# A weight conversion laid out as a pipeline, with batch 0's convolution and some residuals moved to the matrix engine

## The chip, the core and the metric

The kernel runs on one core of a Trainium2 chip. Five engines work beside each other, each through its own queue in order: PE (TensorE, matmuls and their weight loads, shown as PEld), DVE (VectorE), ACT (ScalarE), POOL (GpSimd) and SP (SyncE, here only a queue that issues DMAs). ACT's queue issues DMAs too. The time that counts is the device time of one execution in microseconds. Three runs of the kernel before gave 1051.89, 1057.13 and 1061.42 us; the median is 1057.13 us.

## The reference, cut to what matters

Three stages follow each other, for 4 batches of 576 positions and 512 channels:

```python
scores = scale * np.matmul(q, k.transpose(0, 1, 3, 2))          # 8 heads of 64
kth = np.partition(scores, -32, axis=-1)[..., -32:-31]           # the 32nd largest of each row
attn = softmax(np.where(scores >= kth, scores, -1e9))
x = concat_heads(attn @ v)                                       # (4, 576, 512)

gate = sigmoid(sum(conv_w[k] * xp[:, k:k+S, :] for k in range(5)))   # causal, per channel
x = (gate * (x @ w_val)) @ w_out

u = x + real(fft(fft(x, axis=1), axis=2))
un = layernorm(u)
out = u + relu(un @ w_ch1) @ w_ch2                               # 512 -> 2048 -> 512
```

The five weights (w_val, conv_w, w_out, w_ch1, w_ch2) come as 64-bit floats. The kernel reads them as pairs of 32-bit words and builds a 32-bit float out of each pair; every matrix is then split into a 16-bit high part and a 16-bit low part (the residual), so that three 16-bit matmuls replace one in 32 bits.

## The kernel before, in words

Attention is worked off pair of heads by pair of heads: 16 pairs (4 for each batch), each in five tiles u = 0 to 4 of 128 query rows for two heads (the fifth tile holds both heads' last 64 rows). For a tile PE computes the scores into PSUM (`pss`, L219), ACT copies them out (`ssb`, L220 and L221), and DVE finds the 32 largest of each row: five instructions on halves (L245 to L249), then four rounds of MAX8 (L260) with three of MATCH_REPLACE8 (L269) between them. ACT takes the exponential (L265), DVE masks it by the threshold (L283, one tile later), ACT writes the high part `hl` (L284), and the low part comes from POOL (L285, L292), except that in batch 0 512 of 576 columns of it come from PE: the identity `eye` times the 32-bit e minus the identity times the 16-bit hl (`pe`, L288 and L289), copied out by ACT (L290). A transposing DMA on SP turns hl into `et` (L294), and PE multiplies it with v into `pav` (L316).

At the end of a pair (`attn_finish`) PE spreads the row sums (`pr`, `pt`), ACT copies them (`xt`, L353, L354), DVE normalises (L355), and the causal convolution with five taps follows for the pair's 128 channels: ACT makes the nearest and the farthest tap (L358, L363), DVE adds three taps (L369, 3 instructions in the first three pairs of a batch), POOL adds the farthest (L371, through the helper of L117), and ACT takes the tanh (L372). ACT also copies x out for the following matmul (`xhl` L364, `xt` L365).

Beside attention run, in the slots of the tiles, other units of work: during batch 0 the conversion of the weights (`prelude_units`), during batch b+1 the rest of batch b (`moe_units`); the rest of batch 3 comes last, alone. Each unit of the prelude gets a slot by its position in a list.

The conversion of one unit of 1024 floats in each of 128 partitions: ACT's queue issues the load of 1 MB (L668 or L670) into one of two raw buffers (`bx_pre`, `bz_pre`); two DVE instructions put the mantissa and exponent into `ub`, one of two places in `bx_pre` (L671, L672); ACT makes the sign (L675) and the absolute value (L678); POOL multiplies both in four pieces (L685 to L686 through L117). `wsplit` then adds the split: ACT writes the high part (L692), PE forms the low part as above (`pl`, L697 and L698, two halves), and ACT copies it out (L699). 18 units go through `wsplit` (2 of w_val, 8 of w_ch1, 8 of w_ch2); w_out goes through `p1` with its low part by POOL (L736), and its folded copy `wsd` by POOL as well (L747). conv_w goes through `p0`: its load on SP (L718), three small instructions on DVE (L725, L726, L730) and two on ACT (L728, L729).

The unit's code is written out in one piece: load, mantissa, sign, product, split. The framework's scheduler then orders each engine's instructions by program position and by a time model of its own, puts in the waits, and so moves instructions across each other. A wait on one instruction stops all that stand behind it on that engine.

## Time and profile before

| | |
|---|---|
| median of three runs | 1057.13 us |
| the profiled execution | 1057.91 us |
| its span, first to last instruction | 1054.4 us |
| busy in the span: PE, DVE, ACT, POOL | 881.2, 846.2, 664.3, 565.4 us |
| batch 0's attention with the weight conversion | to about 275 us |
| batches 1, 2, 3 | to about 475, 683, 887 us |
| the rest of batch 3, alone | 887 to 1054 us |

The stages are read from the reciprocal that ends each fourth pair's row sums (L334 and L335 at 275.1, 479.9, 687.5 and 888.1 us). Busy time of an engine is an average over stages with different limits, so the prediction looks at the stage that is changed, from 0 to 275 us, by its own table of windows.

### The profile page before, as it was taken

The page shows a single profiled execution, that of the slowest core. Times are in us where ns is not written, and L with a number is a line of the kernel's source. Part 1 is how long each engine was busy: PE and PEld are TensorE (multiplying, and loading weights), DVE is VectorE, ACT ScalarE, POOL GpSimd, SP SyncE. Part 2 cuts the span into 40 slices and gives each one's busy share as a digit, 9 for nine tenths or more (in the row PEclk, how much of TensorE's full clock was granted, in tenths as well). Part 3 has the DMA queues.
Part 4 walks back from the last instruction along what each step waited for, and adds up shares of the span by engine and source line. Part 5 has one row for each costly group of instructions (what it writes and reads, how often), then busy time and mean ns, then how long its engine had stood idle before and what let it go on. Part 6 is the DMA issues. An engine that isn't in the chain of part 4 may idle for free.

```text
span 1054.4 us, 21240 instructions
## 1 busy us (share of the span) xinstructions
PE 881.2 (84%) x7282; PEld 513.4 (49%) x7282; DVE 846.2 (80%) x2568; ACT 664.3 (63%) x1394; POOL 565.4 (54%) x806
## 2 busy tenths in 40 slices
PE   1277767866789799898998998979979998899996
PEld 0033233322455565544656555446555564558563
DVE  5987979968898999998899998999998997223120
ACT  5587987868756877766669758565785763323020
POOL 1764652524485766755957658559584663641000
PEclk9977888988999999998999999999989999999999
DMA  7698585766536555555364546664464353301000
GB/s 205 162 269 222 128 189 129 181 109 131 103 63 105 97 113 120 100 125 123 82 122 93 116 97 110 138 141 70 99 111 91 83 108 55 80 21 26 21 2 29
DMA packets 308805, 115.18 MB, mean 109 GB/s; under 512 B 297040, under 2 KB 300880, under 8 KB 306384
## 3 DMA queue, kind: packets, MB, share of 16 engines
q1 hardware_dynamic: 303840, 90.24, 43.8%
q10 hardware_dynamic: 4848, 23.50, 6.8%
q8 instruction: 59, 0.97, 0.4%
q14 instruction: 58, 0.48, 0.2%
HBM read 44.49 MB, written 6.82 MB: 49 GB/s over the span
## 4 chain that ended last, share of the span: by engine, by line
DVE 32%; PE 27%; ACT 14%; DMA 12%; issue 6%; POOL 6%; SPq 2%; ACTq 0%; POOLq 0%; DVEq 0%
DVE e L283 7%; PE ph L579 6%; DMA et<-hl 5%; PE po L602 5%; DVE tc L260 5%; DVE ty L269 4%; PE pv L407 3%; DMA stk<-pre 3%; DVE ty L249 2%; POOL hl L292 2%; PE pav L316 2%; ACT hl L284 2%; ACT ssb L220 2%; ACT e L265 2%; PE pd L461 2%
## 5 line engine op out<-in xcount | busy, mean ns | idle before, releaser
L260 DVE MAX8 tc<-ty 128x8 f32<-128x96 f32 (+3 forms) x576 | 229.8, 432 | 2.5 <-DVE e L283 0.5
L579 PE MATMUL ph<-R_un,w 128*128 128x256 f16 (+1 forms) x1536 | 202.3, 290 | 14.0 <-ACT bx_h L583 6.5
L579 PEld LDWEIGHTS <-w 128*128 128x128 f16 x1536 | 148.4, 99 | 62.8 <-issue 21.0
L219 PE MATMUL pss<-stk 128*128 128x512 f16 (+3 forms) x640 | 95.0, 306 | 74.3 <-DVE ty L249 45.0
L284 ACT ACTIVATE hl<-e 128x576 f16<-128x576 f32 x144 | 97.9, 683 | 92.6 <-DVE e L283 70.0
L283 DVE SCALAR_TENSOR_TENSOR e<-ssb,tc,e 128x576 f32<-128x576 f32 x144 | 139.4, 996 | 2.6 <-ACT e L265 2.4
L269 DVE MATCH_REPLACE8 ty<-tc,ty 128x144 f32<-128x144 f32 (+2 forms) x432 | 137.2, 323 | 0.0
L602 PE MATMUL po<-w2f,bx_h 128*128 128x512 f16 x576 | 129.2, 379 | 0.0
L316 PE MATMUL pav<-et,vhl 128*64 128x128 f16 (+1 forms) x2240 | 95.2, 224 | 38.7 <-DMA et<-hl 36.9
L292 POOL TENSOR_TENSOR hl<-e,hl 128x512 f16<-128x512 f32 x108 | 125.0, 1157 | 0.0
L265 ACT ACTIVATE e<-ssb,ngm 128x576 f32<-128x576 f32 x144 | 107.4, 777 | 3.9 <-PE pe L288 1.4
L316 PEld LDWEIGHTS <-vhl 128*64 128x64 f16 x2240 | 72.1, 115 | 77.1 <-issue 72.7
L285 POOL TENSOR_TENSOR hl<-e,hl 128x64 f16<-128x64 f32 x144 | 47.5, 333 | 104.6 <-ACT hl L284 82.3
L163 POOL TENSOR_TENSOR pre<-r,pre 96x384 f16<-96x384 f32 x60 | 60.7, 1020 | 79.5 <-ACT r L162 66.8
L219 PEld LDWEIGHTS <-stk 128*128 128x128 f16 (+1 forms) x640 | 41.4, 104 | 124.3 <-issue 76.2
L602 PEld LDWEIGHTS <-bx_h 128*128 128x128 f16 x576 | 55.1, 98 | 64.9 <-issue 0.6
L220 ACT COPY ssb<-pss 128x1024 f32<-128x1024 f32 (+1 forms) x80 | 73.4, 918 | 10.4 <-PE pss L219 7.9
L580 ACT ACTIVATE bx_h<-ph 128x256 f16<-128x256 f32 (+1 forms) x96 | 38.7, 409 | 55.4 <-PE ph L579 55.2
L407 PE MATMUL pv<-xhl,R_wv 128*128 128x288 f16 x384 | 55.9, 303 | 13.1 <-ACT xt L353 5.0
L156 ACT ACTIVATE pre<-r 96x384 f16<-96x384 f32 x60 | 29.6, 519 | 44.6 <-DMA stk<-pre 16.5
L249 DVE TENSOR_TENSOR ty<-pss,ssb 128x576 f32<-128x576 f32 (+1 forms) x80 | 55.6, 695 | 1.9
L697 PE MATMUL pl<-bx_pre,U_wp 128*128 128x512 f32 x72 | 45.4, 716 | 12.0 <-ACT hl L290 6.4
(186 smaller groups left out, 1705.3 us busy)
## 6 DMA issues: line engine op xcount, KB each, us to landing
bx_pre<-in_moe_w_ch_dram ACTq DMA_DIRECT2D x8, 1024.0 KB, 5.7
bz_pre<-in_moe_w_ch_dram ACTq DMA_DIRECT2D x8, 1024.0 KB, 5.3
r<-in_q_dram SPq DMA_DIRECT2D x32, 144.0 KB, 2.7
r<-in_k_dram SPq DMA_DIRECT2D x31, 144.0 KB, 2.6
stk<-stk SPq DMA_DIRECT2D x60, 72.0 KB, 2.3
vr<-in_v_dram SPq DMA_DIRECT2D x32, 128.0 KB, 2.7
out_dram<-U_u SPq DMA_DIRECT2D x16, 256.0 KB, 2.4
R_wv<-scr_wv SPq DMA_DIRECT2D x3, 1024.0 KB, 5.1
```

The lines of the kernel that those rows point to most:

```text
L219: mm(pss[pr, bank, cs], stk[:, 2 * vv, qs], stk[:, 1, ks], start=(vv == 0), stop=(vv == 1))
L220: nc.scalar.copy(ssb[:, :g, 0:512], pss[:, :g, :])
L260: last = vec.max(out=c[:, cols[i], 8 * r : 8 * r + 8], in_=src[:, i, w])
L265: act(e, ssb[:, i, :], AF.Exp, bias=ngm[:, i : i + 1], scale=SC_EXP)
L269: vec.match_replace(out=y[:, i, w], in_to_replace=c[:, cols[i], 8 * r : 8 * r + 8], in_values=src[:, i, w], imm_value=-1e30,)
L283: done = vec.scalar_tensor_tensor(e, ssb[:, i, :], thr, e, op0=ALU.is_ge, op1=ALU.mult, accum_out=rsum)
L284: act(hl[:, 0:S], e, AF.Copy, bias=0.0, scale=1.0)
L292: pool.tensor_tensor(hl[:, S + D : 2 * S], e[:, 0:512], hl[:, 0:512], op=ALU.subtract)
L316: av = mm(st["pav"][i * D : (i + 1) * D, qs], vhl[:, hv, i, cv, :], rhs, start=(m == 0), stop=(m == len(steps) - 1),)
L407: mm(pv[:, :HS], a, r, start=(n == 0), stop=(n == len(pairs) - 1))
L579: mm(ph[:, :nt], a, r, start=(i == 0), stop=(i == len(pr) - 1))
L602: mm(po, a, r, start=(f == 0 and i == 0), stop=(f == NF - 1 and i == 2))
```

## The change

The conversion is split into `raw_load`, `mant`, and `finish`, and a list `weights` of the 18 units is walked by `wstep(n)`: it issues the split of unit n-1, then mantissa, sign and product of unit n, then the load of unit n+1. There are 19 steps where there were 18 units. In `p1` and `p2` POOL's subtractions give way to `pe_lo`: two matmuls and a copy by ACT for each 512 columns, eight times in all. The three small DVE instructions on conv_w move, in the program, from ahead of `p2` to behind the second `wstep` (`p0b`). In batch 0, for the first three pairs, `attn_finish` makes five diagonal matrices of the taps by ACT, in place of the two tap instructions, and lets PE sum the five shifted products in PSUM (`pc`, 512 and 64 columns), from which ACT takes the tanh in two pieces; the three instructions of DVE and the two of POOL go.

```diff
         vec.tensor_tensor(x, x, xt, op=ALU.mult)
         g = e1[:, hp, :]
         last = KC - 1
+        if b == 0 and hp < NPAIR - 1:
+            dg = [e1[:, hp + 1, j * P : (j + 1) * P] for j in range(last)] + [state[("m", 0)]["dg"]]
+            for j in range(KC):
+                act(dg[j], eye, AF.Copy, bias=0.0, scale=cw[:, hp, j : j + 1])
+            act(xhl[:, 0], x, AF.Copy, bias=0.0, scale=1.0)
+            nc.scalar.copy(xt, x)
+            pool_tt(xhl[:, 1], xt, xhl[:, 0], op=ALU.subtract)
+            for n0, n1 in ((0, 512), (512, S)):
+                pc = ps_m.tile([P, 512], F32, tag="psm", name=f"pc_{hp}_{n0}")
+                for j in range(last, -1, -1):
+                    lo = max(n0, last - j)
+                    mm(pc[:, lo - n0 : n1 - n0], dg[j], xt[:, lo - last + j : n1 - last + j], start=(j == last), stop=(j == 0))
+                act(g[:, n0:n1], pc[:, 0 : n1 - n0], AF.Tanh, bias=0.0, scale=0.5 / SX)
+            return
         act(g, x, AF.Copy, bias=0.0, scale=cw[:, hp, last : last + 1])
         far = 0
         if hp < NPAIR - 1:
...
+        def raw_load(src):
+            raw = (blk["z"] if i else blk["t"])[:, 0:2048].bitcast(I32)
...
                 nc.scalar.dma_start(raw.rearrange("p (c n) -> p c n", c=src.shape[1]), src)
             else:
                 nc.scalar.dma_start(raw, src)
+            words = raw.rearrange("p (n t) -> p n t", t=2)
+            tops = raw.bitcast(F16).rearrange("p (n t) -> p n t", t=4)[:, :, 3]
+            return words, tops, blk["t"][:, 2048 + i * 1024 : 3072 + i * 1024]
+        def mant(words, ub):
+            ui = ub.bitcast(I32)
             vec.tensor_scalar(ui, words[:, :, 1], 3, 0x40000000, op0=ALU.logical_shift_left, op1=ALU.bitwise_xor)
             vec.scalar_tensor_tensor(ui, words[:, :, 0], 29, ui, op0=ALU.logical_shift_right, op1=ALU.bitwise_or)
+        def from_f64(src, ub, scale):
+            words, tops, _ = raw_load(src)
+            mant(words, ub)
+            act(words[:, :, 0], tops, AF.Tanh, bias=0.0, scale=SIGN_SCALE)
             act(ub, ub, AF.Abs, bias=0.0, scale=1.0)
-            if dst is None:
-                pool_tt(ub, ub, sg, op=ALU.mult, parts=4)
-            elif 2 <= blk["n"] <= 4:
+            if blk["n"] == 2:
...
-        def wsplit(src, dst_h, dst_l, scale):
-            ub = from_f64(src, None, 1024, scale)
-            u3 = ub.rearrange("p (c n) -> p c n", c=src.shape[1]) if len(src.shape) == 3 else ub
+        weights = []
+
+        def wstep(n):
+            if n > 0:
+                finish(*weights[n - 1])
+            if n < len(weights):
+                ent = weights[n]
+                words, tops, ub = ent[4]
+                mant(words, ub)
+                sg = words[:, :, 0].bitcast(F32)
+                act(sg, tops, AF.Sign, bias=0.0, scale=1.0)
+                act(ub, ub, AF.Abs, bias=0.0, scale=1.0)
+                pool_tt(ub, ub, sg, op=ALU.mult, parts=4)
+            if n + 1 < len(weights):
+                weights[n + 1].append(raw_load(weights[n + 1][0]))
+
+        def finish(src, dst, scale, then, bufs):
+            ub = bufs[2]
+            dst_h, dst_l = dst()
+            u3 = ub.rearrange("p (c n) -> p c n", c=src.shape[1]) if three_d else ub
             act(dst_h, u3, AF.Copy, bias=0.0, scale=scale)
             for g in range(2):
                 pl = ps_m.tile([P, 512], F32, tag="psm", name=f"pl_{blk['n']}_{g}")
-                mm(pl, state[("m", 0)]["ident"] if scale == 16.0 else state[("m", 0)]["idw2"], ub[:, g * 512 : g * 512 + 512], start=True, stop=False)
+                mm(pl, state[("m", 0)]["ident" if scale == 16.0 else "idw2"], ub[:, gs], start=True, stop=False)
                 mm(pl, state[("m", 0)]["nid"], hs, start=False, stop=True)
                 act(ls, pl, AF.Copy, bias=0.0, scale=1.0)
+            if then:
+                then()
+
+        def pe_lo(dst, full, hi, name):
+            pl = ps_m.tile([P, 512], F32, tag="psm", name=name)
+            mm(pl, eye, full, start=True, stop=False)
+            mm(pl, neye, hi, start=False, stop=True)
+            act(dst, pl, AF.Copy, bias=0.0, scale=1.0)
...
+        def p0b():
...
             act(wohl[:, sl], woF[:, sl], AF.Copy, bias=0.0, scale=1.0)
-            pool.tensor_tensor(wohl[:, 2048 + 1024 * i : 3072 + 1024 * i], woF[:, sl], wohl[:, sl], op=ALU.subtract)
+            for g in range(2):
+                cs = slice(1024 * i + 512 * g, 1024 * i + 512 * g + 512)
+                pe_lo(wohl[:, 2048 + cs.start : 2048 + cs.stop], woF[:, cs], wohl[:, cs], f"po_{i}_{g}")
...
             act(wsd[:, :, 0, :], wt, AF.Copy, bias=0.0, scale=1.0)
-            for i in range(2):
-                sl = slice(2 * i, 2 * i + 2)
-                pool.tensor_tensor(wsd[:, sl, 1, :], wt[:, sl, :], wsd[:, sl, 0, :], op=ALU.subtract)
+            for c in range(NCC):
+                pe_lo(wsd[:, c, 1, :], wt[:, c, :], wsd[:, c, 0, :], f"pt_{c}")
...
+        for i in range(2):
+            src = w_val[256 * i : 256 * i + 256].rearrange("(c p) n -> p c n", p=P)
+            weights.append([src, lambda i=i: wv_dst(i), SWV, wv_save if i else None])
+        for dc in range(NCC):
+            for i in range(2):
+                src = w_ch1[dc * P : (dc + 1) * P, i * 2048 : (i + 1) * 2048]
+                ns = slice(i * 1024, (i + 1) * 1024)
+                weights.append([src, lambda dc=dc, ns=ns: (w1[:, dc, 0, ns], w1[:, dc, 1, ns]), SW1, None])
+        for fp in range(NF // 2):
+            src = w_ch2[fp * 256 : fp * 256 + 256].rearrange("(f p) n -> p f n", p=P)
+            fs = slice(2 * fp, 2 * fp + 2)
+            weights.append([src, lambda fs=fs: (w2[:, fs, 0, :], w2[:, fs, 1, :]), SW2, None])
...
         us.append((0, pi))
-        us.append((1, lambda: pv(0)))
-        us.append((1, lambda: pv(1)))
+        for n in range(2):
+            us.append((1, lambda n=n: wstep(n)))
+        us.append((0, p0b))
         us.append((0, pd))
+        for n in range(2, 11):
+            us.append((1, lambda n=n: wstep(n)))
         for ec in range(NCC):
             us.append((1, lambda ec=ec: p3(ec)))
-        for fp in range(NF // 2):
+        for n in range(11, 19):
+            us.append((1, lambda n=n: wstep(n)))
         return us
```

How the change moves instructions, at the three places that the prediction speaks of. First POOL, early in batch 0, around the output weight (w2f holds it, `pre`, `vhl` and `hl` belong to attention, w_80 is the buffer of w1 and holds the folded copy). Before:

```order
L117 TENSOR_TENSOR w2f<-w2f,bx_pre 128x256 x4
L163 TENSOR_TENSOR pre_2_219<-r_0_2_152,pre_2_219 96x6x64
L163 TENSOR_TENSOR pre_2_219<-r_0_2_154,pre_2_219 96x6x64
L741 TENSOR_TENSOR w_80<-w2f 128x4x255
L742 TENSOR_TENSOR w_80<-w2f 128x4x255
L736 TENSOR_TENSOR w2f<-w2f 128x1024
L199 TENSOR_TENSOR vhl_1_314<-vr_2_230,vhl_1_314 128x320
L736 TENSOR_TENSOR w2f<-w2f 128x1024
L285 TENSOR_TENSOR hl_0_0_0_257<-e_0_0_0_178,hl_0_0_0_257 128x64
L285 TENSOR_TENSOR hl_0_0_1_267<-e_0_0_1_180,hl_0_0_1_267 128x64
```

After the change:

```order
L117 TENSOR_TENSOR w2f<-w2f,bx_pre 128x256 x4
L163 TENSOR_TENSOR pre_2_233<-r_0_2_152,pre_2_233 96x6x64
L163 TENSOR_TENSOR pre_2_233<-r_0_2_154,pre_2_233 96x6x64
L788 TENSOR_TENSOR w_80<-w2f 128x4x255
L789 TENSOR_TENSOR w_80<-w2f 128x4x255
L199 TENSOR_TENSOR vhl_1_337<-vr_2_244,vhl_1_337 128x320
L285 TENSOR_TENSOR hl_0_0_0_271<-e_0_0_0_178,hl_0_0_0_271 128x64
L285 TENSOR_TENSOR hl_0_0_1_281<-e_0_0_1_180,hl_0_0_1_281 128x64
```

The two subtractions of L736 are gone, and the two of L747, which stood right behind these rows, too. DVE's rows at this place are the same in both: the first instruction on conv_w (L725, now L770) stands behind the last one on w_out and ahead of the second tile's L246.

Second DVE, around the fifth tile of the first pair (`ty_0_4`; the rows that read `bx_pre` or `bz_pre` are the conversion). Before:

```order
L260 MAX tc_0_137<-ty_0_4_588 128x8
L269 MATCH_REPLACE ty_0_4_588<-tc_0_137,ty_0_4_588 128x96
L260 MAX tc_0_137<-ty_0_4_588 128x8
L269 MATCH_REPLACE ty_0_4_588<-tc_0_137,ty_0_4_588 128x144
L671 TENSOR_SCALAR bx_pre<-bx_pre 128x1024
L260 MAX tc_0_137<-ty_0_4_588 128x8
L672 SCALAR_TENSOR_TENSOR bx_pre<-bx_pre 128x1024
L269 MATCH_REPLACE ty_0_4_588<-tc_0_137,ty_0_4_588 128x288
L297 TENSOR_REDUCE tc_0_137<-tc_0_137 128x9
L260 MAX tc_0_137<-ty_0_4_588 128x8
L671 TENSOR_SCALAR bx_pre<-bz_pre 128x1024
L672 SCALAR_TENSOR_TENSOR bx_pre<-bz_pre,bx_pre 128x1024
```

After the change:

```order
L283 SCALAR_TENSOR_TENSOR e_0_3_0_513,sums_0_138<-ssb_0_3_351,tc_0_137,e_0_3_0_513 128x576
L688 TENSOR_SCALAR bx_pre<-bz_pre 128x1024
L689 SCALAR_TENSOR_TENSOR bx_pre<-bz_pre,bx_pre 128x1024
L283 SCALAR_TENSOR_TENSOR e_0_3_1_515,sums_0_138<-ssb_0_3_351,tc_0_137,e_0_3_1_515 128x576
L260 MAX tc_0_137<-ty_0_4_608 128x8
L269 MATCH_REPLACE ty_0_4_608<-tc_0_137,ty_0_4_608 128x96
L260 MAX tc_0_137<-ty_0_4_608 128x8
L269 MATCH_REPLACE ty_0_4_608<-tc_0_137,ty_0_4_608 128x144
L260 MAX tc_0_137<-ty_0_4_608 128x8
L269 MATCH_REPLACE ty_0_4_608<-tc_0_137,ty_0_4_608 128x288
L260 MAX tc_0_137<-ty_0_4_608 128x8
L245 TENSOR_TENSOR pss_1_0_597<-pss_1_0_597,ssb_1_0_596 128x288
```

Counted through the list (w_out's two are 0 and 1, w_val's 2 and 3), units 6 and 7 had their mantissa instructions inside this tile. After, unit 5 stands ahead of it, and units 6 and 7 follow in the next tile and the one behind that. The rest of the 18 stays within about one tile of its old place, and the last stands in the fourth tile of the fourth pair in both.

Third PE, at the end of the first pair, while the second pair's tiles run (`pt` ends the row sums, `pe_1` and `pl` are low parts, `pss_1_4` is the score of the second pair's fifth tile). Before:

```order
L350 MATMUL pt_0_936<-neye,rsh_0_916 64x64
L288 MATMUL pe_1_0_994<-e_1_1_0_832,eye 128x512
L289 LDWEIGHTS neye
L289 MATMUL pe_1_0_994<-hl_1_1_0_990,neye 128x512
L288 MATMUL pe_1_1_1004<-e_1_1_1_834,eye 128x512
L289 LDWEIGHTS neye
L289 MATMUL pe_1_1_1004<-hl_1_1_1_1000,neye 128x512
L697 MATMUL pl_0_1039<-bx_pre,U_wp_387 128x512
L219 LDWEIGHTS stk_2_226
L219 MATMUL pss_1_4_1077<-stk_2_226 64x512
```

After the change:

```order
L219 LDWEIGHTS stk_3_592
L219 MATMUL pss_1_4_1108<-stk_3_592 64x64
L369 MATMUL pc_0_974<-xt_0_961,R_wv_409 128x512
L369 MATMUL pc_0_974<-xt_0_961,e_0_932 128x511
L369 MATMUL pc_0_974<-xt_0_961,e_0_932 128x510
L369 MATMUL pc_0_974<-xt_0_961,e_0_932 128x509
L369 MATMUL pc_0_974<-xt_0_961,e_0_932 128x508
L369 MATMUL pc_512_981<-xt_0_961,R_wv_409 128x64
L369 MATMUL pc_512_981<-xt_0_961,e_0_932 128x64 x4
L288 MATMUL pe_1_0_1025<-e_1_1_0_852,eye 128x512
L289 LDWEIGHTS neye
L289 MATMUL pe_1_0_1025<-hl_1_1_0_1021,neye 128x512
```

The ten matmuls of the convolution stand right behind the fifth tile's scores, ahead of the low parts of that pair's second tile, which stood ahead of those scores before. The same is found at the ends of the second and third pairs.

## Rows read from the trace of the kernel before

**Rows 1.** Table of windows: busy us and (instructions), granted clock, DMA share.
```profile
core 0: us, PE busy (x) PEld busy (x) DVE busy (x) ACT busy (x) POOL busy (x), PEclk, DMA share, GB/s
...
42.00:275.00 233.00, 166.31 (x977) 73.41 (x978) 201.84 (x573) 188.47 (x325) 114.44 (x159) 0.84 0.72 165
275.00:475.00 200.00, 177.65 (x1682) 110.35 (x1681) 188.15 (x610) 141.84 (x321) 130.78 (x184) 0.99 0.54 103
475.00:683.00 208.00, 193.43 (x1756) 119.19 (x1756) 194.89 (x620) 144.14 (x323) 139.17 (x197) 0.96 0.54 109
683.00:887.00 204.00, 186.47 (x1692) 113.52 (x1687) 192.93 (x619) 134.75 (x303) 127.93 (x185) 0.97 0.48 96
887.00:1054.00 167.00, 153.01 (x1170) 95.50 (x1168) 39.53 (x104) 36.34 (x90) 35.52 (x59) 0.99 0.15 33
```

**Rows 2.** Waits of DVE, 42 to 275 us: total, times, longest.
```profile
DVE bx_pre L671 <- PE pl L697: 15.9, 4, 7.4
DVE bx_pre L671 <- DMA bx_pre<-in_moe_w_ch_dram: 5.2, 2, 4.0
...
DVE e L369 <- ACT xt L365: 1.1, 1, 1.1
```

**Rows 3.** Waits of PE, 42 to 275 us.
```profile
PE pav L316 <- DMA et<-hl: 18.5, 7, 7.1
```

**Rows 4.** Timeline, 24 to 43 us: start, us, instruction, count.
```profile
26.78 0.20 ACT L728 ACTIVATE w<-w 128x20 int32<-128x20 f16 x1
...
28.25 2.77 POOL L163 TENSOR_TENSOR pre<-r,pre 96x384 f16<-96x384 f32 x2
...
29.30 10.90 DVE L725 TENSOR_SCALAR cw<-w 128x20 int32<-128x20 int32 x1
...
30.98 2.34 POOL L741 TENSOR_TENSOR w<-w2f 128x1020 f32<-128x1020 f32 x1
...
33.27 1.99 POOL L742 TENSOR_TENSOR w<-w2f 128x1020 f32<-128x1020 f32 x1
35.23 2.12 POOL L736 TENSOR_TENSOR w2f<-w2f 128x1024 f16<-128x1024 f32 x1
37.30 0.79 POOL L199 TENSOR_TENSOR vhl<-vr,vhl 128x320 f16<-128x320 f32 x1
38.05 2.12 POOL L736 TENSOR_TENSOR w2f<-w2f 128x1024 f16<-128x1024 f32 x1
...
40.12 0.45 DVE L246 TENSOR_TENSOR ty<-pss,ssb 128x288 f32<-128x288 f32 x1
```

**Rows 5.** Groups by line, 16 to 275 us: count | busy, mean ns | idle before.
```profile
L369 DVE SCALAR_TENSOR_TENSOR e<-pav,cw,e 128x575 f32<-128x575 f32 (+2 forms) x9 | 7.3, 809 | 1.1 <-ACT xt L365 1.1
...
L290 ACT ACTIVATE hl<-pe 128x512 f16<-128x512 f32 x34 | 20.1, 600 | 3.3 <-PE pe L289 3.3
...
L363 ACT ACTIVATE e<-pav,cw 128x572 f32<-128x572 f32 x3 | 2.3, 755 | 0.0
L358 ACT ACTIVATE e<-pav,cw 128x576 f32<-128x576 f32 x3 | 2.2, 750 | 0.0
```

**Rows 6.** Timeline of PE and DVE, at 146 and 223 to 229 us.
```profile
146.54 1.02 PE L697 MATMUL pl<-bx_pre,U_wp 128*128 128x512 f32 x2
147.40 0.38 PE L698 MATMUL pl<-w,U_wp 128*128 128x512 f16 x1
...
223.32 0.85 PE L316 MATMUL pav<-et,vhl 128*64 128x128 f16 x12 [7.11 <-DMA et<-hl]
...
224.99 2.08 PE L697 MATMUL pl<-bx_pre,U_wp 128*128 128x512 f32 x2
226.86 0.63 PE L698 MATMUL pl<-w2f,U_wp 128*128 128x512 f16 x1
...
229.22 0.69 DVE L671 TENSOR_SCALAR bx_pre<-bz_pre 128x1024 int32<-128x1024 int32 x1 [7.41 <-PE pl L697]
```

**Rows 7.** Groups of PE by form, 42 to 275 us.
```profile
L219 PE MATMUL pss<-stk 128*128 128x64 f16 x60 | 13.3, 222 | 0.0
```

**Rows 8.** Timeline of ACT at the start: a copy of the identity.
```profile
2.24 0.29 ACT L783 ACTIVATE U_wp<-eye 128x128 f32<-128x128 f32 x1
```

More of the change, by code (lines that the diff above doesn't have):

```diff
@@ L378, in moe_begin @@
         wvt = mp.tile([P, 2304], F32, tag="R", name=f"R_wv_{b}")
+        st["dg"] = wvt[:, NRW : NRW + P]
         st["wvv"] = wvt[:, :NRW].bitcast(F16).rearrange("p (c h n) -> p c h n", c=NCC, h=2)
@@ L652, in prelude_units @@
         blk = {"n": 0}
-        def from_f64(src, dst, n, scale):
+        def raw_load(src):
             i = blk["n"] % 2
@@ L659, in from_f64 @@
                 blk["z"] = mp.tile([P, NBZ], F32, tag="bz", name="bz_pre")
-            raw = (blk["z"][:, 0 : 2 * n] if i else blk["t"][:, 0 : 2 * n]).bitcast(I32)
-            ub = blk["t"][:, 2048 + i * 1024 : 2048 + i * 1024 + n] if dst is None else dst
-            ui = ub.bitcast(I32)
-            words = raw.rearrange("p (n t) -> p n t", t=2)
-            tops = raw.bitcast(F16).rearrange("p (n t) -> p n t", t=4)[:, :, 3]
+            raw = (blk["z"] if i else blk["t"])[:, 0:2048].bitcast(I32)
             if blk["n"] <= 2:
@@ L670, in from_f64 @@
                 nc.scalar.dma_start(raw, src)
+            words = raw.rearrange("p (n t) -> p n t", t=2)
[3 more added lines that the diff above has]
+            ui = ub.bitcast(I32)
             vec.tensor_scalar(ui, words[:, :, 1], 3, 0x40000000, op0=ALU.logical_shift_left, op1=ALU.bitwise_xor)
             vec.scalar_tensor_tensor(ui, words[:, :, 0], 29, ui, op0=ALU.logical_shift_right, op1=ALU.bitwise_or)
-            if dst is None:
-                sg = words[:, :, 0].bitcast(F32)
-                act(sg, tops, AF.Sign, bias=0.0, scale=1.0)
-            else:
-                act(words[:, :, 0], tops, AF.Tanh, bias=0.0, scale=SIGN_SCALE)
+        def from_f64(src, ub, scale):
+            words, tops, _ = raw_load(src)
+            mant(words, ub)
+            act(words[:, :, 0], tops, AF.Tanh, bias=0.0, scale=SIGN_SCALE)
             act(ub, ub, AF.Abs, bias=0.0, scale=1.0)
-            if dst is None:
-                pool_tt(ub, ub, sg, op=ALU.mult, parts=4)
-            elif 2 <= blk["n"] <= 4:
+            if blk["n"] == 2:
                 vec.scalar_tensor_tensor(ub, words[:, :, 0], scale, ub, op0=ALU.mult, op1=ALU.mult)
@@ L692, in wsplit @@
+        def finish(src, dst, scale, then, bufs):
+            ub = bufs[2]
+            three_d = len(src.shape) == 3
+            dst_h, dst_l = dst()
+            u3 = ub.rearrange("p (c n) -> p c n", c=src.shape[1]) if three_d else ub
             act(dst_h, u3, AF.Copy, bias=0.0, scale=scale)
             for g in range(2):
-                hs = dst_h[:, g] if len(src.shape) == 3 else dst_h[:, g * 512 : g * 512 + 512]
-                ls = dst_l[:, g] if len(src.shape) == 3 else dst_l[:, g * 512 : g * 512 + 512]
+                gs = slice(g * 512, g * 512 + 512)
+                hs, ls = (dst_h[:, g], dst_l[:, g]) if three_d else (dst_h[:, gs], dst_l[:, gs])
@@ L721, in p0 @@
                 )
+        def p0b():
+            cwr = w1f[:, 4096 : 4096 + 4 * NCC * KC].bitcast(I32).rearrange("p (a n t) -> p a n t", a=2, t=2)
             n = NCC * KC
@@ L787, in prelude_units @@
         us.append((0, pi))
-        us.append((1, lambda: pv(0)))
-        us.append((1, lambda: pv(1)))
+        for n in range(2):
+            us.append((1, lambda n=n: wstep(n)))
+        us.append((0, p0b))
         us.append((0, pd))
-        for dc in range(NCC):
-            for i in range(2):
-                us.append(
-                    (
-                        1,
-                        lambda dc=dc, i=i: wsplit(
-                            w_ch1[dc * P : (dc + 1) * P, i * 2048 : (i + 1) * 2048],
-                            w1[:, dc, 0, i * 1024 : (i + 1) * 1024],
-                            w1[:, dc, 1, i * 1024 : (i + 1) * 1024],
-                            SW1,
-                        ),
-                    )
-                )
+        for n in range(2, 11):
+            us.append((1, lambda n=n: wstep(n)))
         for ec in range(NCC):
             us.append((1, lambda ec=ec: p3(ec)))
-        for fp in range(NF // 2):
-            us.append(
-                (
-                    1,
-                    lambda fp=fp: wsplit(
-                        w_ch2[fp * 256 : fp * 256 + 256].rearrange("(f p) n -> p f n", p=P),
-                        w2[:, 2 * fp : 2 * fp + 2, 0, :],
-                        w2[:, 2 * fp : 2 * fp + 2, 1, :],
-                        SW2,
-                    ),
-                )
-            )
+        for n in range(11, 19):
+            us.append((1, lambda n=n: wstep(n)))
         return us
```

18 lines of the change are left out of this document (7 added, 11 removed).

## The prediction

> **What bounds the kernel now.** I read the table of windows first, to see which engine is fullest in each stage. In batches 1 to 3 DVE is busy for 188.15 of 200, 194.89 of 208 and 192.93 of 204 us, and PE runs close behind; at the end PE works alone. In 42 to 275 us, the stage that is changed, nobody is full: DVE 201.84 of 233 us, ACT 188.47, PE 166.31 at a mean granted clock of 0.84, POOL 114.44 [rows 1]. DVE has the most work, so the stage lasts as long as DVE's work (201.84) plus its idle time (31.2).
>
> Then I read DVE's waits in that stage. The reader should see that 15.9 us are the mantissa instruction L671 waiting for PE's `pl` matmuls (four times, once 7.4), 5.2 are the same instruction waiting for the load of its raw buffer, and 1.1 is the convolution waiting for ACT [rows 2]. So 21.1 of 31.2 us of idle time sit ahead of the instruction whose code is rearranged. The mantissa overwrites the `ub` place that the `pl` of two units earlier still reads, so it can't start before that.
>
> Next, what makes `pl` late. PE's own waits name the transposing DMA: `pav` waits 18.5 us for `et`, seven times, up to 7.1 [rows 3]. The timeline at 223 us ties the two: `pav` starts after 7.11 us of waiting, `pl` runs behind it on PE's queue at 224.99, at the lower clock level, and the mantissa starts at 229.22 after 7.41 us [rows 6]. At least the longest of the four waits is thus a chain DMA, `pav`, `pl`, mantissa.
>
> Last, the timeline at the start. DVE's L725, an operation on 20 columns, lasts from 29.30 to 40.20 us; 0.16 to 0.45 us is what neighbours of that kind take. Its data were there, since ACT reads the same words at 26.78. POOL runs without a gap over all that time, and L725 ends with the end of POOL's second L736, 40.17 [rows 4]. I read this as DVE held off by POOL's run, through several instructions.
>
> **The sum, against the profiled execution's 1057.91 us** (0.8 above the median of 1057.13; I make no correction for that).
>
> 1. *POOL's subtractions go.* The order leaves L725 (now L770) at its place in DVE's queue, though the program moves it behind the second unit: in this the change does not do what its code says. But POOL's run loses both L736, 2 x 2.12 us [rows 4]. If L725 ends when POOL's run does, that is **-4.2 us** on DVE's path. Ends: 0, if something else ends the stall, and -10.9, if the stall goes altogether. I take the middle since L163, L741, L742 and L199 still stand in the run without a gap. The Trainium skill, "SBUF — State Buffer", section "Who interferes with whom", says that only the port pair of DVE and GpSimd contends, and that whoever starts first has it for one whole instruction; by this rule DVE would wait for no more than one of POOL's instructions, the stall would have another cause, this term would be 0 and the sum 1048. The row speaks against it: 10.90 us is more than four of POOL's longest instruction there, 2.34.
>
> 2. *DVE's part of the convolution goes.* Nine L369 take 7.3 us, and their 1.1 us of waiting goes with them [rows 5]: 8.4 us in three pair ends. At a pair's end DVE already has the next pair's tiles, so this is work taken off the fullest engine. Where DVE next waits for something that comes no earlier, it is lost. Taken for two pair ends of three, of 7.3: **-4.9**; ends 0 and -8.4.
>
> 3. *The mantissa's waits.* In the new order loads and mantissas stand up to one or two tiles later in DVE's queue around the fifth tile (unit 5 ahead of it, 6 and 7 behind it), so `pl` and the loads have more time. But the split of unit n-1 is issued with the mantissa of unit n, so `pl` also stands later on PE, and it still stands behind `pav`. I take half of 21.1: **-10.5**; ends 0 (the waits reappear) and -21.1 (all go).
>
> 4. *PE's added work.* A 32-bit product of 512 columns is two instructions in the trace (`x2`): 1.02 us for both at the high clock level, 2.08 at the low one; a 16-bit one is 0.38 or 0.63 [rows 6]. The convolution has five products of 512 columns per pair, 5.1 to 10.4, and five of 64. For these the nearest row is a 16-bit one of 64 columns, 0.222 [rows 7]; in two parts each, 10 x 0.2 = 2. That is 7.1 to 12.4 us per pair, 21 to 37 in all. The eight `pe_lo` add 8 x 1.40 = 11.2 to 8 x 2.71 = 21.7. Together 32 to 59. PE has 233 - 166.3 = 66.7 us free [rows 1], so it can hold this; at the upper end it is as full as the stage is long. What counts is place: `pc` stands at each pair end ahead of the low parts `pe_1` of the next pair, on which `hl`, `et` and `pav` wait. DVE works tiles ahead and is the cover. Taken: 1.7 us uncovered per pair end, **+5**; ends 0 (covered) and +29 (rival B).
>
> 5. *ACT.* Added: eight copies like L290's at 0.600 [rows 5], 4.8; 15 diagonals at 0.2 to 0.29 [rows 8], up to 4.4; a second tanh piece per pair, about 0.2 each, from L728's 0.20 [rows 4], 0.7. Gone: L358 and L363, 0.750 and 0.755, three each [rows 5], 4.5. Net about +4 to +5.4 on 188.47 busy of 233. ACT isn't the fullest, but it copies out for all; taken **+1**, ends 0 and +5.4.
>
> 6. *Gone from POOL beside these:* its L747 and the far taps; POOL is busy for 114.44 of 233 us [rows 1], so nothing: 0. *The batches behind:* only the order of neighbours shifts there, and the granted clock is 0.96 to 0.99; 0, within 5 us either way.
>
> Sum: -4.2 - 4.9 - 10.5 + 5 + 1 = -13.6, so 1057.9 - 13.6 = 1044.3, **1044 us**.
>
> **Rivals.**
>
> *A, the waits only move.* `pl` stays behind `pav`, and `pav` behind the DMA. Then term 3 is 0 and whatever DVE saves by term 2 is waited off at the next mantissa. Left are the 4.2 us of term 1: 1053.7, about **1053 to 1054**. For it: the chain at 223 us [rows 6] and the 18.5 us of `pav` for `et` [rows 3]; DMA is busy for 0.72 of that stage [rows 1], the same bytes are loaded. Against it: only one of four waits is traced to `pav`, and 5.2 us are a plain late load, which is issued earlier now. Chance 0.25.
>
> *B, PE becomes the bound at the pair ends.* `pc` runs at the low clock level right after PE waited for DVE's normalised x, 12.4 us per pair, and delays `pe_1`, then `et`, then `pav`, then `pl`, and DVE's mantissa waits for it. At some 9.8 uncovered us per pair end (the mean of 7.1 and 12.4) that is +29 over three. Terms 1, 2 and 5 give -8.1; with no gain in term 3: 1057.9 - 8.1 + 29 = 1079; a third of the waits' gain, 3.5, brings **1076**. It decides when the uncovered part is above 8.1 + 3.5 = 11.6 us, or 3.9 per pair end. For it: the granted clock of 0.84 and waits of 7 us on PE, each with low-clock matmuls behind it. Against it: 66.7 us of PE's time are free. Chance 0.18.
>
> *C, the stall at the start is not POOL's run.* Then L725 waits for something else that comes at about 40 us, such as a transfer, and the two L736 buy nothing: term 1 is 0, 1057.9 - 4.9 - 10.5 + 6 = 1048.5, **1048**. This is what the section of the Trainium skill named in term 1 would make of it. Chance 0.07, since the end of the stall and of POOL's run agree within 0.03 us.
>
> The forecast itself has 0.50.
>
> **How the numbers follow.** The likeliest case gives 1044; its own ends, term by term from half the gains to all of term 3, span about 1030 to 1053. All gains together at their ends would be 1057.9 - 10.9 - 8.4 - 21.1 = 1017.5, which I hold for out of reach. Rival A lies inside, B mostly outside. The range 1024 to 1064 leaves out most of B (0.13) and a little at the lower end (0.07). About 1% (10.6 us) is what a measurement of this kernel can tell from no change. Faster than that, below 1046.5: some 0.45 of the forecast's 0.50, 0.04 of A and 0.03 of C, together 0.52. Within 1%: 0.05 of the forecast, 0.21 of A and 0.04 of C, 0.30. Slower: B, 0.18.
>
> **What would show it.** In the changed kernel: L770 ends about 6.7 us after it starts (10.9 by C); DVE's waits of the mantissa for `pl` and the load come to about 10 us, not 21; DVE's busy time in batch 0 falls by 7; the reciprocal that ends batch 0 (275.1) comes at about 261, and the three batches behind keep their 200, 208 and 204. Wrong would be: `pav` and `pl` waits of the same sum under another name (A); `pc` at over 10 us per pair with `pe` or `hl` waiting behind it, and batch 0 as long as before or longer (B); or a difference that lies behind 275 us.

## The result, and the profile after

The changed kernel takes 1064.32 us (median of 20 runs, 1055.47 to 1069.97) against 1057.16 us before (20 runs, 1050.61 to 1062.81): a ratio of 1.006, 95% interval 1.0036 to 1.0084. It is slower by 0.6%, where 1.2% faster was forecast, and lies just above the stated range of 1024 to 1064. The profiled execution has a span of 1063.2 us, 8.8 more than before. Ratios and intervals leave out runs that are over 1.5% above the fastest of their kernel (below, two of twelve of the pipeline alone and one of ten of the kernel with pieces).

The table says where these 8.8 us lie. Its times are those at which DVE ends the last of the 36 MAX8 instructions of a pair of heads, read from the traces (from the start of the span for the first pair); a count of the same instructions is safer between two orders than the reciprocals of the front table, which the change shifts among them. Every kernel was profiled once, so such a time stands for one execution. Pairs of kernels that differ little in batch 0 agree within some 2 us there (270.7 and 270.9, 260.7 and 263.0 below).

| us | pair 1 | pair 2 | pair 3 | pair 4 | batch 0 | batches 1 to 3 | rest |
|---|---|---|---|---|---|---|---|
| before | 85.2 | 68.2 | 54.0 | 63.2 | 270.7 | 616.5 | 167.2 |
| after | 84.1 | 77.5 | 55.8 | 68.7 | 286.1 | 611.7 | 165.4 |

Batch 0 is 15.4 us longer, what follows 6.6 shorter. In batch 0 DVE is busy for 216.4 us in place of 227.2, and idle for 69.7 in place of 43.5: it is busy for 10.8 us less, of which 4.9 are a hold at 29 us that became shorter (below), and waits 26.2 us more.

The same windows as [rows 1], with the borders moved to the ends of the batches (us from the start, then busy us of PE, PEld, DVE, ACT, POOL, granted clock, DMA share, GB/s):

```profile
42.00:291.00 249.00, 182.53 (x1045) 81.20 (x1044) 191.51 (x551) 189.65 (x338) 100.99 (x150) 0.86 0.69 155
291.00:495.00 204.00, 185.27 (x1701) 114.53 (x1700) 189.93 (x619) 142.65 (x321) 133.35 (x186) 0.97 0.58 104
...
899.00:1063.00 164.00, 151.94 (x1143) 94.97 (x1140) 38.36 (x100) 36.45 (x90) 35.36 (x58) 0.99 0.13 34
```

What DVE and PE wait for in that stage answers to [rows 2] and [rows 3] (total, times, longest):

```profile
DVE e L283 <- ACT e L265: 41.5, 11, 12.2
DVE bx_pre L688 <- DMA bx_pre<-in_moe_w_ch_dram: 3.6, 2, 2.4
DVE bx_pre L688 <- PE pl L731: 3.1, 4, 1.0
```

```profile
PE pav L316 <- DMA et<-hl: 30.9, 10, 9.8
PE pc L369 <- ACT xt L363: 12.3, 2, 8.2
```

The mantissa (L671, now L688) waited 21.1 us and now waits 6.7. In its place stands a wait that had no row of note before: DVE's mask L283 waits 41.5 us for ACT's exponential L265. Of these, 25.1 us lie at the ends of the first three pairs. Another 15.4 lie before 110 us, before any `pc`; the longest, 8.84 us at 105.2, stands behind two transposes of `et` that were issued at 84.20 and 87.29 and took 14.4 and 12.9 us to land, beside a load of 1 MB that took 13.5. Most of the kernels below have such waits before 110 us too.

The timeline at the end of the first pair (start, us, engine, line, in brackets the idle time ahead and what ended it):

```profile
131.12 1.17 PE L219 MATMUL pss<-stk 128*64 128x512 f16 x8 [7.12 <-DVE ty L249]
131.61 0.69 ACT L363 COPY xt<-pav 128x576 f32<-128x576 f32 x1
...
132.35 2.08 PE L369 MATMUL pc<-xt,R_wv 128*128 128x512 f32 x2
134.21 5.11 PE L369 MATMUL pc<-xt,e 128*128 128x511 f32 x8
...
139.16 0.33 PE L369 MATMUL pc<-xt,R_wv 128*128 128x64 f32 x2
139.33 1.06 PE L369 MATMUL pc<-xt,e 128*128 128x64 f32 x8
140.22 1.08 PE L288 MATMUL pe<-e,eye 128*128 128x512 f32 x2
...
141.06 0.94 ACT L156 ACTIVATE pre<-r 96x384 f16<-96x384 f32 x2 [5.69 <-DMA vr<-in_v_dram]
...
142.73 0.57 ACT L370 ACTIVATE e<-pc 128x512 f32<-128x512 f32 x1
...
143.60 0.77 ACT L265 ACTIVATE e<-ssb,ngm 128x576 f32<-128x576 f32 x1
...
144.47 0.82 DVE L283 SCALAR_TENSOR_TENSOR e<-ssb,tc,e 128x576 f32<-128x576 f32 x1 [12.15 <-ACT e L265]
```

`pc` runs from 132.35 to 140.4. Its first 512-column product takes 2.08 us, the lower clock level of [rows 6]; the four others take 5.11 together, since the granted clock is 0.50 until 137.3 and 1.00 from there on. `pe`, which reads the 32-bit e, starts only behind it, at 140.22; the exponential that writes such a buffer next, and that also stands behind the tanh on ACT's queue, starts at 143.60, and DVE has done nothing for 12.15 us. But `pc` is not alone here: ACT itself stands idle for 5.69 us until 141.06, at L156, which prepares the next heads and waits for DMAs (the transpose of `pre`, issued at 132.32, landed at 141.04), and tanh and exponential stand behind that on its queue. Either alone would have held the exponential until 141.5 us or later, so this trace does not give the 12.15 us to `pc` alone. At the second and third pairs' ends it does: the same wait is 4.4 and 8.6 us, with `pc` for 7.8 us each, and ACT waits for `pc` and `pe` themselves:

```profile
201.02 0.60 ACT L370 ACTIVATE e<-pc 128x512 f32<-128x512 f32 x1 [6.85 <-PE pc L369]
...
203.06 0.78 ACT L265 ACTIVATE e<-ssb,ngm 128x576 f32<-128x576 f32 x1 [0.75 <-PE pe L288]
...
203.87 0.82 DVE L283 SCALAR_TENSOR_TENSOR e<-ssb,tc,e 128x576 f32<-128x576 f32 x1 [4.39 <-ACT e L265]
```

At the start, DVE's 20-column instruction against POOL's run, to be held against [rows 4]:

```profile
28.78 6.00 DVE L770 TENSOR_SCALAR cw<-w 128x20 int32<-128x20 int32 x1
...
30.45 2.34 POOL L788 TENSOR_TENSOR w<-w2f 128x1020 f32<-128x1020 f32 x1
...
32.76 1.99 POOL L789 TENSOR_TENSOR w<-w2f 128x1020 f32<-128x1020 f32 x1
34.70 0.45 DVE L246 TENSOR_TENSOR ty<-pss,ssb 128x288 f32<-128x288 f32 x1
34.71 0.79 POOL L199 TENSOR_TENSOR vhl<-vr,vhl 128x320 f16<-128x320 f32 x1
```

It is shorter by 4.90 us (10.90 to 6.00) and ends with L789, whose end is 34.75. It does not last to the end of POOL's run: L199 follows without a gap, and DVE comes through ahead of it, where before it was held through L199 as well.

### The profile page after: what moved, and what is told of

Its sections match the earlier page's. It is cut to its first block, busy times and chain, and to the rows that moved or that the text cites. A ratio compares the mean times of both kernels' runs of the same rounds, so it can differ in the third digit from the quotient of the medians.

```text
span 1063.2 us, 21407 instructions
## 1 busy us (share of the span) xinstructions
PE 908.5 (85%) x7366; PEld 526.5 (50%) x7366; DVE 833.7 (78%) x2559; ACT 669.7 (63%) x1414; POOL 544.1 (51%) x796
## 4 chain that ended last, share of the span: by engine, by line
PE 41%; DVE 20%; DMA 14%; ACT 12%; issue 7%; POOL 5%; SPq 2%; ACTq 0%; POOLq 0%; DVEq 0%
PE po L617 9%; PE ph L594 8%; DMA et<-hl 8%; DVE e L283 4%; DVE tc L260 4%; PE pav L316 3%; PE pu L512 3%; PE pv L422 3%; DVE ty L269 3%; PE pss L219 3%; PE pd L480 2%; ACT hl L284 2%; PE pd L476 2%; POOL hl L292 2%; DMA stk<-pre 2%
## 5 line engine op out<-in xcount | busy, mean ns | idle before, releaser
L283 DVE SCALAR_TENSOR_TENSOR e<-ssb,tc,e 128x576 f32<-128x576 f32 x144 | 138.4, 987 | 41.6 <-ACT e L265 41.5
L285 POOL TENSOR_TENSOR hl<-e,hl 128x64 f16<-128x64 f32 x144 | 47.7, 332 | 134.0 <-ACT hl L284 106.7
L265 ACT ACTIVATE e<-ssb,ngm 128x576 f32<-128x576 f32 x144 | 108.5, 777 | 8.6 <-PE pe L288 4.7
L163 POOL TENSOR_TENSOR pre<-r,pre 96x384 f16<-96x384 f32 x60 | 61.7, 1037 | 84.8 <-ACT r L162 84.0
L219 PEld LDWEIGHTS <-stk 128*128 128x128 f16 (+1 forms) x640 | 41.5, 104 | 80.2 <-issue 22.9
L220 ACT COPY ssb<-pss 128x1024 f32<-128x1024 f32 (+1 forms) x80 | 73.5, 919 | 11.9 <-PE pss L219 10.6
L156 ACT ACTIVATE pre<-r 96x384 f16<-96x384 f32 x60 | 29.7, 518 | 43.1 <-DMA stk<-pre 14.6
L422 PEld LDWEIGHTS <-R_wv 128*128 128x128 f16 x384 | 39.4, 105 | 29.4 <-issue 16.0
```

Source lines behind the costliest of these rows:

```text
L219: mm(pss[pr, bank, cs], stk[:, 2 * vv, qs], stk[:, 1, ks], start=(vv == 0), stop=(vv == 1))
L220: nc.scalar.copy(ssb[:, :g, 0:512], pss[:, :g, :])
L265: act(e, ssb[:, i, :], AF.Exp, bias=ngm[:, i : i + 1], scale=SC_EXP)
L283: done = vec.scalar_tensor_tensor(e, ssb[:, i, :], thr, e, op0=ALU.is_ge, op1=ALU.mult, accum_out=rsum)
L422: mm(pv[:, :HS], a, r, start=(n == 0), stop=(n == len(pairs) - 1))
```

## The experiments

**Theory 1:** the convolution's products on PE stand ahead of `pe` at three pair ends and hold back exponential and DVE; the rest of the change gains. **Rival:** the pipeline only turns the mantissa's waits into others (its loads collide with the transposes of et), and the convolution costs little. Four kernels take the change apart. Ratios are to the kernel before, on the same chip.

**The change without the convolution on PE**

```diff
-        if b == 0 and hp < NPAIR - 1:
-            dg = ...
...
-            return
```

> The change without the convolution on PE (the taps are on DVE, ACT and POOL as before). Theory 1 (the convolution's products stand on PE's queue at three pair ends, hold back pe, so the exponential, so DVE's L283, 25.1 us in the changed kernel, against 7.3 us of L369 saved): the 25 go and the 7 come back, so 1064 - 18 = about 1046, 1040 to 1052; batch 0 ends near 268 us. Rival (the waits come from the pipeline and the collision of its loads with the et transposes, whatever PE does): 1060 to 1070, and waits of L283 for the exponential of 30 us or more stay.

Measured: 1055.82 us, 0.9971 (0.9946 to 0.9996); batch 0 ends at 260.1, and L283 waits 11.2 us for the exponential, all of it ahead of 82 us. As theory 1 has it, batch 0 gets shorter with the convolution gone, by 26.0 us, and the waits at the pair ends go; but that is 8 us more than theory 1 gave (near 268), which is what the kernel with the diagonals alone adds back, below. The total fell less than expected, since batches 1 to 3 took 624.6 us in place of 611.7; what happens there is told below.

**The convolution on PE alone**, put into the kernel before:

```diff
+        if b == 0 and hp < NPAIR - 1:
+            dg = ...
...
+            return
```

> The kernel before with the convolution of the first three pairs on PE alone. Theory 1: +18, so about 1075 (1068 to 1085), with waits of L283 for the exponential of 15 to 30 us in 42 to 291 us. Rival (pipeline and loads are the cause): 7 us are saved on DVE and little is lost, 1050 to 1060.

Measured: 1086.39 us, 1.0264 (1.0224 to 1.0303); batch 0 ends at 290.9, 20.2 later than before. L283 waits 32.1 us for the exponential; both are a little above what was expected. The convolution is thus dear with or without the pipeline, and the rival falls as the account of these 26 us. The collision that it names is there all the same, in the 8.84 us at 105.2 and in the next kernel.

**The output weight's low parts on PE alone**

```diff
-            pool.tensor_tensor(wohl[...], woF[:, sl], wohl[:, sl], op=ALU.subtract)
+            for g in range(2):
+                pe_lo(wohl[...], woF[:, cs], wohl[:, cs], f"po_{i}_{g}")
```

> The kernel before with the eight low parts of the output weight on PE alone. Both theories: the stall of the 20-column instruction at 29 us falls from 10.9 to about 6 us, so -4 to -5, about 1053; if the wait for L283 at 61 and 66 us (5.9 in the changed kernel) comes from these products, it is 1057 to 1060. By the rule that DVE waits for no more than one POOL instruction the stall would not change: 1057.

Measured: 1061.86 us, 1.0045 (1.0013 to 1.0076). The stall is 6.01 us as expected, but the total is above all three figures, and the first pair ends at 87.5 and not at 85.2: in it the mantissa waits 12.3 us in place of 3.0. The gain is given back within the same pair (SP's queue, PE and DVE):

```profile
63.72 11.93 SPq L294 DMA_TRANSPOSE et<-hl  x1
75.54 1.07 PE L316 MATMUL pav<-et,vhl 128*64 128x128 f16 x16 [10.48 <-DMA et<-hl]
78.89 0.69 DVE L671 TENSOR_SCALAR bx_pre<-bz_pre 128x1024 int32<-128x1024 int32 x1 [10.86 <-PE pl L697]
```

`pav` waits for a transpose that was issued at 52.20 and took 23.3 us to land, `pl` stands behind `pav`, and the mantissa behind `pl`. A load of 1 MB issued at 53.37 took 18.1 us; before, a transpose issued at 52.06 took 3.3 us and the load at 57.46 5.0. The kernel without the convolution has the same stretch with another wait:

```profile
63.32 11.91 SPq L294 DMA_TRANSPOSE et<-hl  x1
75.15 0.68 ACT L284 ACTIVATE hl<-e 128x576 f16<-128x576 f32 x1 [12.01 <-DMA et<-hl]
75.17 1.12 PE L316 MATMUL pav<-et,vhl 128*64 128x128 f16 x17 [10.73 <-DMA et<-hl]
...
77.11 0.82 DVE L283 SCALAR_TENSOR_TENSOR e<-ssb,tc,e 128x576 f32<-128x576 f32 x1 [8.06 <-ACT e L265]
```

A transpose of et holds SP's queue for 11.91 us, ACT's copy into `hl` waits for the one ahead of it (issued at 52.20, 22.9 us), the exponential stands behind that, and DVE waits. In both kernels the first pair waits for transfers; why these take so long there is not shown. The DMA engines' share of 42 to 88 us is 0.99 and 0.94, and 0.89 before.

**The pipeline alone** (POOL keeps the low parts, DVE the convolution):

```diff
-        if b == 0 and hp < NPAIR - 1:
...
-                pe_lo(wohl[...], woF[:, cs], wohl[:, cs], f"po_{i}_{g}")
+            pool.tensor_tensor(wohl[...], woF[:, sl], wohl[:, sl], op=ALU.subtract)
```

> The conversion as a pipeline alone (low parts of the output weight on POOL, convolution on DVE as before). Theory 1: the mantissa's waits fall from 21 to 7 us and little takes their place: 1043 to 1052. Rival: the waits come back as waits for et or the exponential, 1055 to 1065.

Measured: 1050.7 us, 0.9929 (0.9893 to 0.9965), the fastest kernel of the study, 1.3% below the change. Batch 0 ends at 260.7; the mantissa waits 8.7 us in place of 21.1, L283 1.7 for the exponential. With the low parts on PE as well (above) it ends at 260.1: those are worth nothing in it. The first pair alone ends at 80.7 here and at 88.6 there.

Next, what it is about the convolution: its place ahead of `pe`, or its price.

**One tile later, and two tiles later**

```diff
-            for n0, n1 in ((0, 512), (512, S)):
+            def late():
+                for n0, n1 in ((0, 512), (512, S)):
...
+            conv_late.append([1, late])    # [2, late] in the second
```

> The change with the products of the convolution and its tanh issued one tile later (the diagonals and the copies of x stay); on PE they then stand behind pe of the second pair's second tile and behind the scores, not ahead of pe. Place theory (the cost is that pe, and so the exponential, stands behind products that wait 8 us for x): the waits of L283 for the exponential in 84 to 291 us fall from 34.8 to under 15 us, batch 0 ends near 268, total 1045 to 1052. Price theory (some 8 us of PE at the low clock for each pair, wherever they stand): the 25 us stay within 6, 1058 to 1066.

> The same with two tiles' delay, on PE behind the scores of the second pair's next tile. Place theory: as with one tile, 1045 to 1052, or a little more where the tanh now stands ahead of other exponentials. Price theory: 1058 to 1066.

Measured: 1066.98 us, 1.0128 (1.0075 to 1.0181), and 1065.64 us, 1.0079 (1.0048 to 1.0111). Batch 0 ends at 277.0 and 275.4, 9 and 11 us earlier, and L283 waits 25.4 and 15.4 us for the exponential. Before 110 us these waits are as before (15.9 and 14.8 us, 15.4 in the change); after it 9.5 and 0.7 us are left of 26.0, so the wait that the place theory names is mostly gone. But both totals are above what that theory gave, since other waits take its place: in the second kernel DVE waits 8.9 us after 110 us for ACT's copies of the scores and 6.9 for `pl`. Nor did these two edits change the place alone: at the later place `pc` ran at the higher clock level throughout (granted clock 1.00, against 0.69 to 0.71 in the change) and kept PE busy for 5.6 to 5.9 us per pair instead of 7.8 to 8.0, 6.6 us less in all.

**Products in 16 bits, at the same place**

```diff
-            dg = [...]
+            dg = [t.bitcast(F16)[:, 0:P] for t in [...]]
...
-                    mm(pc[...], dg[j], xt[...], ...)
+                    mm(pc[...], dg[j], xhl[:, 0, ...], ...)
```

> The change with the convolution's products in 16 bits (taps and x rounded to their high parts; the low parts are left out), at the same place on PE ahead of pe. A 512-column product is then 0.38 to 0.63 us and not 1.02 to 2.08, so about 3 us per pair in place of 8, and it needs the 16-bit copy of x, which ACT makes one instruction earlier. Price theory: 12 to 18 of the 25 us go, 1046 to 1052. Place theory (waiting for x is what holds pe): under 10 go, 1054 to 1062.

Measured: 1053.76 us, 0.9971 (0.994 to 1.0002). `pc` takes 2.6 us per pair and batch 0 ends at 272.6, 13.5 earlier, as the price theory has it; the total is 2 us above its figure:

```profile
129.98 0.61 PE L369 MATMUL pc<-xhl,R_wv 128*128 128x512 f16 x1
130.38 1.91 PE L369 MATMUL pc<-xhl,e 128*128 128x511 f16 x4
...
132.36 1.11 PE L288 MATMUL pe<-e,eye 128*128 128x512 f32 x2
```

**The products twice**

```diff
-                for j in range(last, -1, -1):
+                for j in list(range(last, -1, -1)) * 2:
```

> The change with each 512-column and 64-column product of the convolution issued twice into the same PSUM (the sum is then twice the convolution). PE has some 8 us more for each of the three pairs at the same place. If PE's time there is exposed in full: batch 0 ends 20 to 25 us later than in the change (286.1), at 306 to 311, and the total is about 1085. If half of it is covered by the wait: 296 to 300, about 1075. If PE's free time in the stage takes it: under 290, about 1065.

Measured: 1092.28 us, 1.0311 (1.0259 to 1.0364); `pc` takes 13.5, 12.5 and 17.5 us, 19.9 more than in the change, and batch 0 ends at 304.6, 18.5 later, just short of the first branch. L283 waits 54.5 us for the exponential, 47.7 of them at the three pair ends (25.1 in the change, 11.7 with 16 bits). So 93% of the added time of PE is seen at the end.

**The diagonals alone**

```diff
             dg = ...
             for j in range(KC):
                 act(dg[j], eye, AF.Copy, bias=0.0, scale=cw[:, hp, j : j + 1])
-            ...
-            return
```

> The change with the convolution on DVE, ACT and POOL as before, but ACT still makes the 15 diagonal matrices, which nothing reads. If ACT's added copies carry part of the cost: batch 0 ends 4 us or more later than without the convolution on PE (260.1), at 264 or later. If it is PE alone: 258 to 263, and the total is within 5 us of 1056.

Measured: 1064.02 us, 1.0039 (1.0013 to 1.0066); batch 0 ends at 268.0, 7.9 after the kernel without the convolution on PE. The 15 copies take 0.40 us each, 6.0 in all, where 0.29 was assumed from [rows 8]. That they cause the 7.9 us is not shown: DVE's waits after 100 us are 10.2 us for `pl` and only 2.6 for ACT's copy of x, which stands behind the diagonals on its queue.

Against this kernel the change is 18.1 us longer in batch 0. That fits the timelines: 25.1 us of waits at the pair ends, less the 7.3 of DVE's taps, are 17.8.

These kernels stand in a line by PE's time for `pc` in batch 0, all with pipeline, low parts on PE and diagonals:

| `pc`, us in three pairs | 0 | 7.8 | 23.6 | 43.5 |
|---|---|---|---|---|
| batch 0 ends at, us | 268.0 | 272.6 | 286.1 | 304.6 |

(The first keeps DVE's taps, some 7.3 us of work, the others don't.) From the second to the fourth the end moves by 32.0 us for 35.7 us of PE (of the 43.5, 1.4 are other work of PE in between).

**16 bits and one tile later**

```diff
-            dg = [...]
+            dg = [t.bitcast(F16)[:, 0:P] for t in [...]]
...
+            def late():
...
+                        mm(pc[...], dg[j], xhl[:, 0, ...], ...)
+            conv_late.append([1, late])
```

> The change with the convolution's products both in 16 bits (low parts of taps and x left out) and one tile later. Place and price add: one tile later gave 9 us in batch 0, 16 bits 13.5; together batch 0 ends at 264 to 267, and the total is about 1045, if no long hold of an L283 falls into batches 1 to 3. If both remove the same wait: 270 to 273, 1052.

Measured: 1068.18 us, 1.0098 (1.0061 to 1.0135); batch 0 ends at 274.8. A miss by 8 us: place and price don't add. `pc` keeps PE busy for only 4.6 us in the three pairs there, L283 waits 2.3 us for the exponential after 110 us, and yet batch 0 ends later than with 16 bits at the old place. PE's wait for et rose to 42.4 us, and DVE's for `pl` after 110 us to 11.4.

**The stall at the start.** Two kernels ask whether POOL's run is what holds DVE.

The pipeline alone with conv_w converted later:

```diff
-        us.append((0, p0))
...
-        us.append((0, p0b))
...
+            if n == 2:
+                us.append((0, p0))     # its load now waits for wsd
+            if n == 3:
+                us.append((0, p0b))
```

> The pipeline alone with the conversion of conv_w moved out of POOL's run (its load waits for the folded output weight; its DVE instructions stand in the fourth tile). If POOL's gapless run holds DVE's 20-column instruction: it takes 0.2 us or one POOL instruction there, and 10.7 us of DVE time go at the start. If DVE's time decides in the first pair: 1040; if the transposes of et on the DMA queues decide there, the first pair ends as in the pipeline alone (80.7 us) or later and the total stays at 1048 to 1053.

Measured: 1051.14 us, 0.9959 (0.9923 to 0.9996), not to be told from the pipeline alone. The first pair ends 2.4 us earlier (78.3), batch 0 2.3 later (263.0). The 20-column instruction takes 0.18 us, at 86.95. At its old place another DVE instruction is held:

```profile
30.03 9.48 DVE L283 SCALAR_TENSOR_TENSOR e<-ssb,tc,e 128x576 f32<-128x576 f32 x1
```

```profile
30.45 2.34 POOL L772 TENSOR_TENSOR w<-w2f 128x1020 f32<-128x1020 f32 x1
32.75 1.99 POOL L773 TENSOR_TENSOR w<-w2f 128x1020 f32<-128x1020 f32 x1
34.71 4.19 POOL L767 TENSOR_TENSOR w2f<-w2f 128x1024 f16<-128x1024 f32 x2
```

An L283 takes 0.81 us elsewhere; this one ends at 39.51, 0.6 behind POOL's run (38.90). So the hold does not belong to conv_w.

The kernel before with POOL's long instructions in pieces:

```diff
-            pool.tensor_tensor(wt[:, :, 1 : NE - 1], ...)
+            pool_tt(wt[:, :, 1 : NE - 1], ..., parts=5)      # and three more, parts=4 or 5
```

> The kernel before with the four long POOL instructions beside DVE's 20-column one (L741, L742, both L736) cut into pieces of at most 0.7 us (18 instructions, no gap between them). If POOL's gapless run holds DVE whatever the length of its pieces, L725 still takes about 10 us. If DVE gets its turn at the end of the POOL instruction that is running, L725 takes under 1.5 us once the pieces begin, so at most about 3 us (after the 1.4 us of L163 that runs then). Total 1052 to 1060 by the first.

Measured: 1059.11 us, 0.9994 (0.9968 to 1.002). Here L725 came through in 0.88 us, with the end of the L163 that was running (29.85) and ahead of the pieces, and L726, the next on conv_w, was held through a second L163 and all 18 of them:

```profile
30.17 10.98 DVE L726 SCALAR_TENSOR_TENSOR cw<-w,cw 128x20 int32<-128x20 int32 x1
```

```profile
30.68 3.92 POOL L117 TENSOR_TENSOR w<-w2f 128x204 f32<-128x204 f32 x7
34.56 2.54 POOL L117 TENSOR_TENSOR w2f<-w2f 128x256 f16<-128x256 f32 x4
37.06 1.55 POOL L117 TENSOR_TENSOR w<-w2f 128x204 f32<-128x204 f32 x3
38.57 2.54 POOL L117 TENSOR_TENSOR w2f<-w2f 128x256 f16<-128x256 f32 x4
```

## Why the prediction was wrong

- **Term 4, PE's added work, is the step that failed.** It took +5 us, 1.7 per pair end, because "DVE works tiles ahead and is the cover" and PE had 66.7 us free in the stage. The convolution on PE costs batch 0 26.0 us (286.1 against 260.1), net of the taps that DVE is rid of; 18.1 of them are the products and their tanh (286.1 against 268.0, where the diagonals are made too). The duration of `pc` was right (7.1 to 12.4 forecast per pair, 7.8 to 8.0 measured). What failed is the cover: there is next to none, since the runs with `pc` at 7.8, 23.6 and 43.5 us show nearly all of it at the end. Free time of PE in the sum of a stage says nothing of a place at which the chain scores, maxima, exponential, `pe` comes round to PE.
- **Rival B** had the price (+29 over three pair ends), but another way. It went by `et`, `pav` and `pl` to the mantissa; measured is `pc`, `pe` and tanh, exponential, L283. The mantissa's waits stayed short all the same, which is one reason why the time is not B's 1076; the batches and the rest behind batch 0, 6.6 us shorter, are another.
- **Term 3** was right in direction, and in time near its size: the pipeline alone brings batch 0 10.0 us, where the term took 10.5. The waits fell further than it said, to 8.7 us there and 6.7 in the change, not 10.6.
- **Term 1** was near by its row, -4.9 for -4.2, and the reading that POOL's run holds DVE through several instructions was right. That the stall ends with the run was not: it ended ahead of L199, which is the difference of 0.7 us. Rival C falls, since the stall moved with POOL's instructions. The rule of the Trainium skill ("SBUF — State Buffer", "Who interferes with whom"), that who has the shared ports keeps them for one whole instruction, does not cover these holds: 10.98 us went by through 18 pieces of at most 0.67. For most of the L283 it fits, as the last section counts. But the gain did not last: with the low parts on PE, the first pair ends about as late as before or later (84.1 in the change, 87.5 with them alone, 88.6 without the convolution, against 85.2 before and 80.7 in the pipeline alone); in the second and third of these a transpose of `et` is late. The term should have asked what is late next.
- **Term 2**: DVE's 7.3 us of work went. It is inside the 26.0.
- **Term 5** sized ACT's diagonals at 0.29 us and took +1; the copies take 0.40 us each, and in the kernel with the diagonals alone batch 0 ends 7.9 us later. One pair of kernels shows it, with two different orders, so its size is uncertain by some us, and its cause is not shown.
- **Batches 1 to 3**: "0, within 5 us" came out for the change, 4.8 us shorter, but by luck. They lasted 611.7 to 631.4 us in the fourteen kernels, whose work there is the same.

Open: how much of the 26.0 is place and how much price. The later place gave 9 and 11 us back, but `pc` was also 6.6 us shorter there; at the rate of the table (32.0 us for 35.7) that alone would be some 6 us, an estimate, which leaves 3 to 5 for the place. The 16-bit products gave 13.5, both together 11.3, and every edit also shifts the order around it. Open too is how much of the first pair's 12.15 us is `pc` and how much the transfer that ACT waits for.

## What to carry to other kernels

Before work is moved to an engine with free time, find the chain that returns to that engine every tile and ask on which side of it the new work will stand: at that place nearly its whole duration can count, whatever the engine's share. Take a change of several parts as several changes: here the pipeline alone was worth -0.7% (0.9929), and the part that took work off the fullest engine turned it into +0.6%. And when a stall is removed, price what ends next in that stage before counting the gain.
